# Attention of every tile in float32 quarters of the array, first mixture in blocks of 512 tokens, memory laid out anew

## The chip, the core and the metric

The kernel runs on one core of a Trainium2 chip. The metric is the device time of one execution in microseconds (us); smaller is better. The engines are named as in the profile: PE (TensorE, matmuls; PEld is its weight load), DVE (VectorE), ACT (ScalarE), POOL (GpSimd) and SP (SyncE, which here issues DMAs). Each has its own queue, worked off in order, and they meet at semaphores.

## The reference

Inputs and outputs are float32 in the reference. Three stages follow each other, for 8 x 576 = 4608 tokens of 512 features:

```python
# attention inside chunks of 64 tokens, 8 heads of 64
scores = scale * np.matmul(q_c, k_c.transpose(0, 1, 2, 4, 3))
scores = scores - np.max(scores, axis=-1, keepdims=True)
attn = np.exp(scores)
attn = attn / (np.sum(attn, axis=-1, keepdims=True) + 1e-09)
out = np.matmul(attn, v_c)
# first mixture: 512 -> 768 three times, the maximum of them, 768 -> 512
h = np.maximum(np.maximum(x @ w1, x @ w2), x @ w3)
x = h @ w_out
# second mixture: each token goes to one of 8 experts, 512 -> 1024 -> 512
e_idx = np.argmax(x @ w_gate, axis=1)
out[mask] = gate_w[mask, None] * eom[mask, e, None] * (np.maximum(x[mask] @ w1[e], 0.0) @ w2[e])
```

The gate's weight is the softmax's value at the chosen expert, `eom` a sigmoid of a second set of logits. The first mixture's four weight matrices reach the chip as float64 words.

## The kernel before, in words

**Tiles and blocks.** A tile is 128 tokens (two chunks of 64, all eight heads); there are 36. The first mixture takes three tiles together, as a block of 384 tokens; there are 12 blocks (`blocks`, line 62). The second mixture takes blocks of 256 tokens of one expert, gathered from a table in memory.

**Hi and lo.** A float32 matmul is made of three float32r ones: each operand is split in a hi part (an ACT copy that rounds) and a lo part (a subtraction on DVE or POOL), and `mm3` (lines 99 to 102) adds hi x hi, hi x lo and lo x hi. All matmuls of both mixtures are of this kind.

**Attention** has five steps per tile. `att_Q` loads q and k (SP) and, from tile 5 on, splits them: q into `qs`, k into `kb`, in which k stands as blocks so that one matmul does two heads and two chunks. `att_S` makes the scores. From tile 5 on these are four `mm3` of 128x256 columns, twelve matmuls, into the PSUM banks `a2` (line 427). Tiles 0 to 4 (`a < NF`) take plain float32 instead, in quarters of the array: 16 matmuls of 64x64, one per head and chunk (line 417), which need no parts. ACT then copies the scores to `e`, DVE and POOL take off the maximum, ACT takes the exponential, DVE sums, POOL multiplies by the inverse. `att_P` loads v (and splits it, from tile 5 on), transposes the probabilities on PE (four matmuls, line 465) and copies them to SBUF: to `pTF` in the first tiles, and to `pT` in hi and lo parts from tile 5 on (four ACT copies, four DVE subtractions). `att_V` makes the values in the same two ways (line 495 for quarters, line 508 for `mm3`), again in `a2`, and splits the result into `xt`, the first mixture's input (two `xt`, used by blocks in turn).

**First mixture.** `convert` (lines 529 to 548) turns one 512x128 part of a weight matrix from float64 words into hi and lo: an ACT operation, four DVE operations (lines 537, 539, 542, 544), an ACT copy and a POOL subtraction. There are 18 such parts (`conv_w`) and six of `moe_w_out` (`conv_o`, which also works out the gates' weights on PE). Three buffers `cy` are used in turn by all 24. The float64 words of the 18 parts are staged in `wst`, six at a time, which lies in the memory of `wo`, the converted `moe_w_out`. `moe_f` makes one of 18 groups of a block: 12 matmuls of 128x384 into one of three PSUM banks in turn; ACT and DVE form the maximum over three groups in `hs0`, and ACT and POOL split it into `ht[g]`. `moe_y` makes the outputs of a tile, in two halves of 18 matmuls (256 and 272 columns; the second with the gate's logits). `gate` works out the routing of a block, and `rows_out` writes the rows to the scratch tensor.

**Order.** All this is listed as operations with an engine, an estimated duration, a priority and the keys of the memory that they read and write. `order` (line 282) then runs a list schedule: each engine takes the most urgent operation that can start by the estimates, and that is the fixed order of its queue. So attention of block j + 1, the mixture of block j and the conversions are interleaved by priorities (`v0(j)` plus constants), and the dependencies follow the order of the list. Operations on a made-up engine `HOST` hand memory over: they come when all its old users are done.

**Second mixture.** Its first block is planned with the rest (`early_half`, `late_half`), the others follow in a written-out order (`step`). Buffers for the experts' weights (`raw`) take over the memory of attention, regions R0 to R3.

The lines that say it best are these two groups of the scores:

```python
for hp in range(HP):                       # tiles 0 to 4: 16 float32 matmuls
    add("PE", 0.44, pr + 1, [...], [...], lambda hp=hp: mm(hp))
...
for hp in range(HP):                       # tiles 5 to 35: 12 float32r matmuls
    add("PE", t_mm(256), pr + 1, ["qsh", "qsl"] + kbk, pk, lambda hp=hp: mm3(...))
```

## Time and profile before

| | us |
|---|---|
| median of 3 runs | 1287.7 |
| lowest and highest of them | 1287.33, 1288.24 |
| span of the profiled execution, first to last instruction | 1284.5 |
| busy: PE, DVE, ACT, POOL | 1236.8, 642.9, 523.2, 351.3 |
| first mixture with attention and conversion, by PE's timeline | 0 to 799.8 |
| second mixture | 799.8 to 1284.5 |

The profiled execution's own device time is not given apart; its span stands for it, 3.2 us under the median of the runs. A matmul's duration in the profile runs to its modelled end and overlaps the next one's; what one costs is the distance from its start to the next start. The busy time of PE therefore says only that it had something under way. Waits are told from the view that lists who waited for whom. A line number such as L97 or L100 is often that of a helper (97 is every subtraction, 100 to 102 the three matmuls of `mm3`); the tiles beside it tell which one is meant. Buffer numbers are left out: `a` is `a2`, `mm` any of three banks, `U` a region that several buffers share.

### The profile page before, as it was taken

To read this page: it belongs to the slowest core of one execution; us is meant where nothing else is said; L and a number is where in the kernel's file an instruction comes from. 1 tells how busy PE (TensorE), PEld (TensorE's weight loads), DVE (VectorE), ACT (ScalarE), POOL (GpSimd) and SP (SyncE) were. 2 spreads that over 40 slices of the span, in tenths; PEclk is the share of its full clock that TensorE was granted. 3 is DMA by queue.
4 is the path that set the end of the run, shared out by engine and by line. 5 is a ranking of instruction groups with operands and counts; after the bars stand their busy time and mean duration, and the time that the engine had idled before them with its cause. 6 is when DMAs were issued, how large, how long until landed. Compare 5 with 4: busy or idle time off the path is not lost. (4 is left out here: it accounts for less than half of the span.)

```text
span 1284.5 us, 22188 instructions
## 1 busy us (share of the span) xinstructions
PE 1236.8 (96%) x8450; PEld 1188.8 (93%) x8450; DVE 642.9 (50%) x1397; ACT 523.2 (41%) x1055; POOL 351.3 (27%) x376
## 2 busy tenths in 40 slices
...
PEclk7888999999999999999999999999999999999998
...
GB/s 284 194 97 84 65 27 75 33 68 50 50 59 42 66 34 75 25 75 26 75 9 35 131 25 41 199 34 54 47 107 200 216 59 34 115 108 42 59 162 29
DMA packets 54107, 102.98 MB, mean 80 GB/s; under 512 B 5983, under 2 KB 15199, under 8 KB 53984
## 3 DMA queue, kind: packets, MB, share of 16 engines
...
q14 instruction: 54, 0.44, 0.1%
...
## 5 line engine op out<-in xcount | busy, mean ns | idle before, releaser
L100 PE MATMUL mm<-xt,wpc 128*128 128x384 f32 x768 | 264.0, 344 | 2.1 <-DVE hs L616 1.9
L101 PE MATMUL mm<-xt,wpc 128*128 128x384 f32 x768 | 261.3, 340 | 3.2 <-DVE xt L97 3.2
L102 PE MATMUL mm<-xt,wpc 128*128 128x384 f32 x768 | 261.1, 340 | 0.0
L873 DVE SCALAR_TENSOR_TENSOR wo<-mm,wo 128x512 fp32r<-128x512 f32 x64 | 43.6, 689 | 238.6 <-ACT wo L869 191.9
L100 PEld LDWEIGHTS mm<-xt,wpc 128*128 128x128 f32 x768 | 145.8, 190 | 3.6 <-DVE hs L616 2.1
L101 PEld LDWEIGHTS mm<-xt,wpc 128*128 128x128 f32 x768 | 145.7, 190 | 3.6 <-DVE xt L97 3.6
L102 PEld LDWEIGHTS mm<-xt,wpc 128*128 128x128 f32 x768 | 145.5, 189 | 0.0
L97 POOL TENSOR_TENSOR ht<-hs,ht 128x384 fp32r<-128x384 f32 x72 | 74.4, 1033 | 255.5 <-ACT ht L618 254.6
L889 POOL DMA_INDIRECT out_dram<-yo,S x42 | 44.1, 1051 | 354.9 <-ACT yo L886 271.4
L616 DVE TENSOR_TENSOR hs<-mm,hs 128x384 f32<-128x384 f32 x144 | 80.1, 556 | 121.7 <-PE mm L102 117.2
L100 PE MATMUL mm<-wo,ht 128*128 128x256 f32 (+1 forms) x432 | 125.4, 290 | 0.0
L102 PE MATMUL mm<-wo,ht 128*128 128x256 f32 (+1 forms) x432 | 123.0, 285 | 0.0
L101 PE MATMUL mm<-wo,ht 128*128 128x256 f32 (+1 forms) x432 | 123.0, 285 | 0.0
L618 ACT CAST ht<-hs 128x384 fp32r<-128x384 f32 x72 | 36.9, 513 | 204.7 <-DVE hs L616 203.9
L100 PE MATMUL tr<-wpc,wo 128*128 128x512 f32 x304 | 120.3, 396 | 0.0
L102 PE MATMUL tr<-wpc,wo 128*128 128x512 f32 x304 | 118.6, 390 | 0.0
L101 PE MATMUL tr<-wpc,wo 128*128 128x512 f32 x304 | 118.5, 390 | 0.0
L97 DVE TENSOR_TENSOR pT<-tr,pT 64x256 fp32r<-64x256 f32 x124 | 52.3, 422 | 72.8 <-ACT pT L478 71.5
L869 ACT ACTIVATE wo<-mm 128x512 fp32r<-128x512 f32 x64 | 38.2, 597 | 122.5 <-PE mm L102 120.0
L886 ACT ACTIVATE yo<-tr,xg 128x512 f32<-128x512 f32 x42 | 28.5, 687 | 143.0 <-PE tr L102 143.0
L97 DVE TENSOR_TENSOR wpc<-raw,wpc 128x512 fp32r<-128x512 f32 x112 | 70.3, 685 | 30.7 <-ACT wpc L827 30.7
L101 PEld LDWEIGHTS mm<-wo,ht 128*128 128x128 f32 x432 | 81.8, 189 | 0.0
...
## 6 DMA issues: line engine op xcount, KB each, us to landing
...
```

Of the source, the lines that this page charges most:

```text
L97: eng.tensor_tensor(out=o, in0=a, in1=b, op=ALU.subtract)
L100: PE.matmul(o, ah, bh, start=first, stop=False)
L101: PE.matmul(o, ah, bl, start=False, stop=False)
L102: PE.matmul(o, al, bh, start=False, stop=last)
L616: add("DVE", t_dve(N), up, [pk, hk], [hk], lambda: DVE.tensor_tensor(out=h, in0=ps, in1=h, op=ALU.max))
L618: add("ACT", t_act(N), up, [hk], [("ht", g, 0)], lambda: ACT.copy(ht[g][:, 0, :N], h))
L869: ACT.activation(out=hT()[:, 0, 2 * c:2 * c + 2], in_=l1_ps(c), func=ACTF.Relu)
L873: DVE.scalar_tensor_tensor(out=hT()[:, 1, fs], in0=l1_ps(c), scalar=0.0, in1=f(hT()[:, 0, fs]), op0=ALU.max, op1=ALU.subtract)
L886: ACT.activation(out=yo(b, t), in_=ps_y[t], func=ACTF.Copy, scale=xg(b)[:, t, DM:DM + 1])
L889: POOL.indirect_dma_start(out=out, out_offset=bass.IndirectOffsetOnAxis(ap=ic[b % 4]()[:, t, 1:2].bitcast(U32), axis=0), in_=yo(b, t), in_ ...
```

## The change

All 36 tiles take attention in float32 quarters; the hi and lo parts of q, k, v and the probabilities, their buffers (`kb`, `pT`, `qs`, `vs`) and their clearing go, and PE's operation for a tile's scores or values is planned as one of 0.7 us. Blocks have four tiles, so that `moe_f` has 512 columns; there are nine. Memory is laid out anew: R0 to R3 hold q, k, v (three v buffers), three score buffers, two probability buffers and two of the three `cy`; `xt` is split into hi and lo tiles; the float64 words are staged, four parts at a time, in the place of the second `xt`, which is handed over (`HOST`) when all 18 parts are read; `wo` has its own memory from the start. The second mixture's `xs[0]` and other late buffers get new places of the same use. Priorities are set for the longer blocks (`VB`, `FD`, `YD`), and tiles 3 and 4 lose their own (`AF`). The rest of the diff removes comments.

```diff
-    blocks = [3] * 12
+    blocks = [4] * 9
...
     LP, LQ = -158, 8
-    AO, AS = -15, 14
+    AO, AS = -15, 16
-    AF, PS, VS, GP, YB = -40, 19, 0, 54, 1
+    AF, PS = -40, 19
+    VB, FD, YD = 76, 3.0, 56
...
-    NF, NE2, NW = 5, 3, 3
-    S0, S1, Q0, Q1, K0, K1, MULD = 2, 36, 0, 9, 3, 9, 2
+    NE2, NW = 3, 3
+    S0, S1, MULD = 2, 36, 2
...
-    kb = ar.tile([P, 2, 4, 2, P], F32R, tag="R0", name="kb")
-    pT = ar.tile([P, 2, 2, 4, P], F32R, tag="R1", name="pT")
-    qk_a = ar.tile([P, 2, 2, HP, P], F32, tag="R2", name="qk_a")
-    qkv_b = ar.tile([P, 4, HP, P], F32, tag="R3", name="qkv_b")
-    qk_buf = [qk_a[:, 0], qk_a[:, 1], qkv_b[:, 0:2]]
-    v_buf = [qkv_b[:, 2], qkv_b[:, 3]]
-    qvs = buf([P, 2, 2, 4, P], F32R, "qvs")
-    qs, vs = qvs[:, 0], qvs[:, 1]
-    e = buf([P, H, 64], F32, "e")
-    mxs, sms = ([buf([P, H], F32, f"{n}{i}") for i in range(4)] for n in ("mx", "sm"))
-    xt = [buf([P, 2, KD, TB * P], F32R, f"xt{i}") for i in range(2)]
+    rg = [ar.tile([P, 2048], F32, tag=f"R{n}", name=f"rg{n}") for n in range(4)]
+    part = lambda n, i, m: rg[n][:, i * 512:(i + m) * 512]
+    qk_buf = [part(n, i, 2).rearrange("p (w h t) -> p w h t", w=2, h=HP) for n, i in ((0, 0), (0, 2), (1, 0))]
+    v_buf = [part(n, i, 1).rearrange("p (h t) -> p h t", h=HP) for n, i in ((1, 2), (1, 3), (2, 3))]
+    es = [part(2, i, 1).rearrange("p (h j) -> p h j", h=H) for i in range(3)]
+    pTF = [part(3, i, 1).rearrange("p (a b c) -> p a b c", a=HP, b=2) for i in range(2)]
+    NV = len(v_buf)
+    xtn = lambda hl, i: f"xt{'hl'[hl]}{i}"
+    xtile = lambda hl, i: p1.tile([P, KD, TB * P], F32R, name=xtn(hl, i), tag=xtn(hl, i))
+    xt = [[xtile(hl, 0) for hl in range(2)], None]
+    wst = [p1.tile([P, 2, KD, P, 2], I32, name=f"wst{hl}", tag=xtn(hl, 1)) for hl in range(2)]
...
-    wst = wp.tile([P, 6, KD, P, 2], I32, tag="wo", name="wst")
-    wo_t = []
-    US = 4096
+    wo_t = [wp.tile([P, 2, NG, DM + 2 * E], F32R, tag="wo", name="wo")]
...
     so = [View(i * 1024, 1024, I32, "p (k f w) -> p k f w", k=KD, w=2) for i in range(2)]
-    cy = [View(2048 + i * 512, 512, I32, "p (k f) -> p k f", k=KD) for i in range(3)]
-    wT = [View(3584, 512, F32, "p (k f) -> p k f", k=KD)]
-    es = [e] + [View(o, 512, F32, "p (h j) -> p h j", h=H) for o in (3584, 1024, 1536)]
-    pTF = [View(i * 512, 512, F32, "p (a b c) -> p a b c", a=HP, b=2) for i in range(2)]
+    wT = [View(2048, 512, F32, "p (k f) -> p k f", k=KD)]
+    cyv = View(2560, 512, I32, "p (k f) -> p k f", k=KD)
+    cy = [(cyv.ap, cyv)] + [
+        (part(3, 2 + i, 1).bitcast(I32).rearrange("p (k f) -> p k f", k=KD), ("cy", i)) for i in range(2)
+    ]
...
     def e_of(a):
-        i = a % NE2 if a < NF else 0
-        return (es[i].ap if i else e), [es[i] if i else ("e", 0), ("mx", i), ("sm", i)], mxs[i], sms[i]
+        i = a % NE2
+        return es[i], [("e", i), ("mx", i), ("sm", i)], mxs[i], sms[i]
...
+    T_Q = 0.7
     def att_Q(a, pr):
-        t = qk_buf[a % 3]
         for w in range(2):
             load(a, w, pr - LA)
-        if a < NF:
-            return
-        add("ACT", t_act(512), pr, [("qk", a % 3, 0)], ["qsh"], lambda: ACT.copy(qs[:, 0], t[:, 0]))
-        add_sub(lo((Q0, Q1), a), 512, pr, [("qk", a % 3, 0), "qsh"], ["qsl"], qs[:, 1], t[:, 0], f(qs[:, 0]))
-        for h2 in range(2):
-            sl = h64(h2)
-            add("ACT", t_act(512), pr, [("qk", a % 3, 1)], [("kbh", h2)],
-                lambda sl=sl, h2=h2: ACT.copy(kb[sl, 0, :, h2], t[sl, 1]))
-        for h2 in range(2):
-            sl = h64(h2)
-            add_sub(lo((K0, K1), a), 512, pr, [("qk", a % 3, 1), ("kbh", h2)], [("kbl", h2)],
-                    kb[sl, 1, :, h2], t[sl, 1], f(kb[sl, 0, :, h2]))
...
     def att_S(a, pr):
         e, (ek, mk, sk), mx, sm = e_of(a)
-        if a < NF:
...
+        t = qk_buf[a % 3]
+        bank = [ps[:, i] for ps, _, hs in quarters(a) for i in range(hs.stop - hs.start)]
+        def mm():
+            for hp in range(HP):
                 for h2 in range(2):
                     for c in range(2):
                         x = t[h64(h2), :, hp, h64(c)]
                         PE.matmul(bank[h2][h64(c), hp], x[:, 0], x[:, 1], start=True, stop=True)
...
-        else:
-            kbk = [("kbh", 0), ("kbh", 1), ("kbl", 0), ("kbl", 1)]
-            pk = ["a2"]
-            sc = ps_a2.rearrange("p (a h c j) -> p a h c j", a=HP, h=2, c=2)
-            for hp in range(HP):
...
-            for c in range(2):
-                sl = h64(c)
-                add("ACT", t_act(512), pr + 1, pk + ([ek] if c else []), [ek] if c == 0 else [("e", 1)],
-                    lambda sl=sl, c=c: ACT.copy(e[sl], sc[sl, :, :, c, :].rearrange("p a h j -> p (a h) j")))
-        add("DVE", t_dve(512), pr + 1, [ek, ("e", 1)], [mk], lambda: DVE.tensor_reduce(out=mx, in_=e, axis=AX.X, op=ALU.max))
+        add("PE", T_Q, pr + 1, [("qk", a % 3, 0), ("qk", a % 3, 1)], [x for _, kk, _ in quarters(a) for x in kk], mm)
+        for ps, pk, hs in quarters(a):
+            add("ACT", t_act(256 * (hs.stop - hs.start)), pr + 1, pk + ([ek] if hs.start else []), [(ek, 1)] if hs.start else [ek],
+                lambda ps=ps, hs=hs: ACT.copy(e.rearrange("p (a b) j -> p b a j", b=2)[:, hs], ps))
+        ek2 = [ek, (ek, 1)]
+        add("DVE", t_dve(512), pr + 1, ek2, [mk], lambda: DVE.tensor_reduce(out=mx, in_=e, axis=AX.X, op=ALU.max))
...
     def att_P(a, pr):
         e, (ek, _, _), _, _ = e_of(a)
         load(a, 2, pr - LV)
-        vv = v_buf[a % 2]
-        if a >= NF:
-            add("ACT", t_act(512), pr + 6, [("v", a % 2)], ["vsh"], lambda: ACT.copy(vs[:, 0], vv))
-            add("POOL", t_pool(512), pr + 6, [("v", a % 2), "vsh"], ["vsl"], lambda: sub(POOL, vs[:, 1], vv, f(vs[:, 0])))
         pp = ps_tr[a % 2].rearrange("p (a c i) -> p a c i", a=HP, c=2)
 
...
-        add("PE", 0.43, pr + 2, [ek], [("tr", a % 2)], fn)
+        add("PE", 0.45, pr + 2, [ek], [("tr", a % 2)], fn)
         x = pTF[a % 2]
-        d = lambda hl, c, h2: x.ap[h64(c), :, h2] if a < NF else pT[h64(c), hl, h2, :, 64 * c:64 * c + 64]
         for i, (c, h2) in enumerate((c, h2) for c in range(2) for h2 in range(2)):
-            kf = [x, ("pTF", a % 2, 0)] if i == 0 else [("pTF", a % 2, i)]
-            add("ACT", t_act(256), pr + 2, [("tr", a % 2)] + ([("pTF", a % 2, 0)] if a < NF and i else []),
-                kf if a < NF else [("pth", c, h2)],
-                lambda c=c, h2=h2: ACT.copy(d(0, c, h2), pp[h64(h2), :, c]))
-        for c in range(2) if a >= NF else ():
-            for h2 in range(2):
-                add_sub("DVE", 256, pr + 2, [("tr", a % 2), ("pth", c, h2)], [("ptl", c, h2)],
-                        d(1, c, h2), pp[h64(h2), :, c], f(d(0, c, h2)))
+            add("ACT", t_act(256), pr + 2, [("tr", a % 2)], [("pTF", a % 2, i)],
+                lambda c=c, h2=h2: ACT.copy(x[h64(c), :, h2], pp[h64(h2), :, c]))
...
     def att_V(a, pr):
         j, t_ = tile_block[a]
-        dst = xt[j % 2][:, :, :, t_ * P:(t_ + 1) * P]
+        dst = lambda hl: xt[j % 2][hl][:, :, t_ * P:(t_ + 1) * P]
         xk = lambda hl: [("xt", j % 2, t_, hl, h2) for h2 in range(2)]
...
+        vv, x = v_buf[a % NV], pTF[a % 2]
+        bank = [ps[:, i] for ps, _, cs in quarters(a) for i in range(cs.stop - cs.start)]
+        def mm():
+            for hp in range(HP):
                 for c in range(2):
                     for h2 in range(2):
-                        PE.matmul(bank[c][h64(h2), hp], vv[h64(c), hp, h64(h2)], x.ap[h64(c), hp, h2], start=True, stop=True)
...
-            return
-        ptk = [(x, c, h2) for x in ("pth", "ptl") for c in range(2) for h2 in range(2)]
-        pk = ["a2"]
-        pv = ps_a2.rearrange("p (a h c) -> p a h c", a=HP, h=2)
-        for hp in range(HP):
-            add("PE", t_mm(256), pr + 3, ["vsh", "vsl"] + ptk, pk, lambda hp=hp: mm3(
-                pv[:, hp], vs[:, 0, hp], vs[:, 1, hp], pT[:, 0, :, hp], pT[:, 1, :, hp], True, True,
-            ))
-        for h2 in range(2):
-            sl = h64(h2)
-            add("ACT", t_act(512), pr + 3, pk, [xk(0)[h2]], lambda sl=sl, h2=h2: ACT.copy(dst[sl, 0], pv[sl, :, h2]))
-        for h2 in range(2):
-            sl = h64(h2)
-            add_sub("DVE", 512, pr + 3, pk + [xk(0)[h2]], [xk(1)[h2]], dst[sl, 1], pv[sl, :, h2], f(dst[sl, 0]))
+                        PE.matmul(bank[c][h64(h2), hp], vv[h64(c), hp, h64(h2)], x[h64(c), hp, h2], start=True, stop=True)
+        add("PE", T_Q, pr + 3, [("v", a % NV)] + [("pTF", a % 2, i) for i in range(4)], [x for _, kk, _ in quarters(a) for x in kk], mm)
+        o = lambda hl: dst(hl).rearrange("p a (b i) -> p b a i", b=2)
+        for ps, pk, cs in quarters(a):
+            n = 256 * (cs.stop - cs.start)
+            kx = lambda hl: [("xt", j % 2, t_, hl, i) for i in range(cs.start, 2)] if n == 256 else xk(hl)
+            add("ACT", t_act(n), pr + 3, pk, kx(0), lambda ps=ps, cs=cs: ACT.copy(o(0)[:, cs], ps))
+            add("DVE", t_dve(n), pr + 3, pk + kx(0), kx(1), lambda ps=ps, cs=cs: sub(DVE, o(1)[:, cs], ps, f(o(0)[:, cs])))
...
     def conv_w(n, pr):
         g, w = divmod(n, 3)
-        t = wst[:, n % 6]
-        tk = [("wo", 2 * (n % 6)), ("wo", 2 * (n % 6) + 1)]
+        t = wst[n % 4 // 2][:, n % 2]
+        tk = [("ws", n % 4)]
         add("SP", 1.46, min(pr - 25, LP + LQ * n), [], tk, lambda: SP.dma_start(
...
-        pc, x = wpc[n // 4], xt[j % 2]
+        pc, x = wpc[n // 4], lambda: xt[j % 2]
         for kk in range(KD):
             add("PE", t_mm(N), pr, [("w", n, 0), ("w", n, 1)] + xt_keys(j), [pk], lambda kk=kk: mm3(
                 ps, pc[:, 0, n % 4, kk], pc[:, 1, n % 4, kk],
-                x[:, 0, kk, :N], x[:, 1, kk, :N], kk == 0, kk == KD - 1), lead=0.1)
+                x()[0][:, kk, :N], x()[1][:, kk, :N], kk == 0, kk == KD - 1), lead=0.1)
...
     def v0(j):
-        return 25 + 64 * j
+        return 25 + VB * j
...
     akeys = [
-        [(x, h2) for x in ("kbh", "kbl") for h2 in range(2)],
-        [(x, c, h2) for x in ("pth", "ptl") for c in range(2) for h2 in range(2)],
         [("qk", i, w) for i in range(2) for w in range(2)],
         [("qk", 2, 0), ("qk", 2, 1), ("v", 0), ("v", 1)],
+        [x for i in range(3) for x in (("e", i), (("e", i), 1))] + [("v", 2)],
+        [("pTF", i, x) for i in range(2) for x in range(4)] + [("cy", i) for i in range(2)],
     ]
...
     def attention(a, n):
         def prio(i):
             j, t = tile_block[i]
-            return -100 + PS * i if j == 0 else AF + AO + AS * i if i < NF else v0(j - 1) + AO + AS * t
+            return -100 + PS * i if j == 0 else v0(j - 1) + AO + AS * t
...
-            if i == NA - 1 and VS:
-                att_V(i, pr[i])
             if i + 1 < NTILE:
                 att_S(i + 1, pr[i + 1])
-            if i != NA - 1 or not VS:
-                att_V(i, pr[i])
-    add("POOL", 1.7, -60, [], [(x, h2) for x in ("kbh", "kbl") for h2 in range(2)], lambda: zero(POOL, kb))
-    add("POOL", 1.7, -55, [], [(x, c, h2) for x in ("pth", "ptl") for c in range(2) for h2 in range(2)], lambda: zero(POOL, pT))
-    NA = max(NF, blocks[0])
+            att_V(i, pr[i])
+    NA = blocks[0]
     attention(0, NA)
     for n in range(NFT):
         conv_w(n, v0(0) + CW * n - CO)
     add("SP", 0.5, 0, [], ["gwr"], gw_load, lat=LD)
-    add("HOST", 0.0, 0, [], [("wo", i) for i in range(2 * NG)],
-        lambda: wo_t.append(wp.tile([P, 2, NG, DM + 2 * E], F32R, tag="wo", name="wo")))
+    add("HOST", 0.0, 0, [], [("ws", i) for i in range(4)] + xkeys(1, 0, 1),
+        lambda: xt.__setitem__(1, [xtile(hl, 1) for hl in range(2)]))
     for i in range(NG):
         conv_o(i, v0(0) + CP + i)
...
         for n in range(NFT):
-            moe_f(j, n, base + 2.75 * n)
+            moe_f(j, n, base + FD * n)
         if j == NB - 1:
-            early_half(base + 44)
-        for i, half in enumerate((0, 1) if j < YB else (1, 0)):
+            early_half(base + YD - 6)
+        for i, half in enumerate((0, 1) if j == 0 else (1, 0)):
             for t in range(blocks[j]):
-                moe_y(j, t, half, base + 50 + 2.2 * t + 6.6 * i)
+                moe_y(j, t, half, base + YD + 2.2 * t + 8.8 * i)
             if half:
-                gate(j, base + GP + 6.6 * i)
-        rows_out(j, base + 60)
-    late_half(pe_ + 62)
+                gate(j, base + YD + 4 + 8.8 * i)
+        rows_out(j, base + YD + 12)
+    late_half(pe_ + YD + 12)
     for o in order():
         o.fn()
```

## Rows read from the trace of the kernel before

**Rows 1.** Page, part 2, PEclk: granted TensorE clock in tenths, 40 equal slices of the span.
```profile
PEclk7888999999999999999999999999999999999998
```
**Rows 2.** Busy time by stretch: PE, PEld, DVE, ACT, POOL (records), granted clock, DMA share, GB/s.
```profile
30.00:122.00 92.00, 69.90 (x452) 65.70 (x450) 88.58 (x128) 49.95 (x95) 59.40 (x46) 0.87 0.41 135
...
136.00:800.00 664.00, 663.60 (x4431) 661.07 (x4431) 377.53 (x961) 294.78 (x641) 173.05 (x185) 1.00 0.16 51
```
**Rows 3.** PE's waits, 130 to 860 us, all of them: total us, times, longest.
```profile
PE a L845 <- DMA xg<-x_scratch,S: 0.4, 1, 0.4
```
**Rows 4.** Timeline of PE: start, us, instruction; block 0, block 1, second mixture.
```profile
35.52 0.69 PE L101 MATMUL mm<-xt,wpc 128*128 128x384 f32 x1 [3.17 <-DVE xt L97]
...
135.46 0.34 PE L100 MATMUL mm<-xt,wpc 128*128 128x384 f32 x1
...
799.76 0.28 PE L100 MATMUL mm<-qvs,wpc 128*128 128x256 f32 x1
```
**Rows 5.** Timeline of PE, first and last of 118 such starts in block 11.
```profile
760.05 0.34 PE L100 MATMUL mm<-xt,wpc 128*128 128x384 f32 x1
...
780.64 0.34 PE L100 MATMUL mm<-xt,wpcr 128*128 128x384 f32 x1
```
**Rows 6.** Timeline of PE, second mixture: first of 23 512-column matmuls, next start behind them.
```profile
818.66 0.40 PE L101 MATMUL tr<-wpc,wo 128*128 128x512 f32 x1
...
823.91 0.28 PE L100 MATMUL mm<-wo,wpc 128*128 128x256 f32 x1
```
**Rows 7.** Timeline of PE: first of twelve matmuls of a tile's scores, next start.
```profile
300.91 0.28 PE L100 MATMUL a<-kb,qvs 128*128 128x256 f32 x1
...
302.34 0.29 PE L100 MATMUL mm<-wo,ht 128*128 128x272 f32 x1
```
**Rows 8.** Timeline of PE around tile 3's values, in quarters.
```profile
43.76 0.34 PE L102 MATMUL mm<-xt,wpc 128*128 128x384 f32 x1
44.03 0.69 PE L495 MATMUL a<-U,qkv_b 64*64 64x64 f32 x32
44.65 0.66 PE L465 MATMUL tr<-ident,U 128*128 128x128 f32 x4
45.06 0.42 PE L100 MATMUL mm<-xt,wpc 128*128 128x384 f32 x1
```
**Rows 9.** Timeline of PE: tile 4's values, with the wait before them.
```profile
64.06 1.14 PE L495 MATMUL a<-U,qkv_b 64*64 64x64 f32 x32 [4.95 <-ACT e L439]
```
**Rows 10.** Timeline of DVE: last step of weight 17, and of the last part of moe_w_out.
```profile
92.51 0.68 DVE L544 SCALAR_TENSOR_TENSOR U<-wst,U 128x512 int32<-128x512 int32 x1
...
120.87 0.69 DVE L544 SCALAR_TENSOR_TENSOR U<-U 128x512 int32<-128x512 int32 x1
```
**Rows 11.** Instructions of line 539: ns at the shortest, in the median, at the longest.
```profile
L539 DVE TENSOR_SCALAR U<-U x24: 409/1138/1510, 12.2 to 117.9; 128x512 int32<-128x512 int32 x24
```
**Rows 12.** Groups of DVE, 0 to 122 us: busy us, mean ns, idle before.
```profile
L539 DVE TENSOR_SCALAR U<-U 128x512 int32<-128x512 int32 x24 | 23.2, 974 | 0.1
L537 DVE TENSOR_SCALAR U<-U 128x512 f32<-128x512 f32 x24 | 17.2, 728 | 3.0 <-ACT U L536 3.0
L544 DVE SCALAR_TENSOR_TENSOR U<-wst,U 128x512 int32<-128x512 int32 x18 | 16.3, 905 | 0.0
L542 DVE SCALAR_TENSOR_TENSOR U<-wst,U 128x512 int32<-128x512 int32 x18 | 15.7, 877 | 0.1
```
**Rows 13.** Groups of POOL, 0 to 122 us.
```profile
L97 POOL TENSOR_TENSOR kb<-qk_a,kb 64x512 fp32r<-64x512 f32 x4 | 5.6, 1406 | 0.2
L97 POOL TENSOR_TENSOR qvs<-qkv_b,qvs 128x512 fp32r<-128x512 f32 x3 | 4.4, 1470 | 0.4 <-ACT qvs L459 0.3
```
**Rows 14.** Busy time of PE alone, in block 11's outputs: length, busy (records), clock, DMA, GB/s.
```profile
785.20:792.80 7.60, 7.60 (x63) 1.00 0.24 65
```
**Rows 15.** Timeline of PE: the gate's two small matmuls in block 11.
```profile
794.54 0.18 PE L671 MATMUL psg<-ohz,tri 128*128 128x32 bf16 x1
794.57 0.18 PE L672 MATMUL psg<-ohc,ones_b 128*128 128x32 bf16 x1
```

58 lines of the change are left out of this document (17 added, 41 removed).

## The prediction

> **What bounds the kernel now.** I read the page's slices first, then the busy time by stretch, then the tensor engine's waits, and last its timeline, where costs are taken from start to start, because the durations of pipelined matmuls overlap. The granted clock is below full only in the first slices and the last [rows 1]. By stretch there are two regimes. From 136 to 800 us PE is busy 663.6 of 664.0 us at clock 1.00 while DVE works 377.5, ACT 294.8 and POOL 173.1 us [rows 2], and the list of PE's waits from 130 to 860 us holds one entry, 0.4 us [rows 3]: there only PE's own work counts. From 30 to 122 us it is the other way round: DVE is busy 88.6 of 92 us, PE 69.9 at a granted clock of 0.87 [rows 2] (a mixture of the 1.2 and the 2.4 GHz level). That is the conversion of the float64 weights, which feeds block 0. Block 0's matmuls run from 35.5 us, block 1 begins at 135.46 and the second mixture at 799.76 us [rows 4]. What follows 799.76 (484.7 us) does the same instructions after the change and I leave it as it is.
>
> So there are two accounts: PE's work from block 1 to the second mixture, and the time at which block 1 can begin.
>
> **First mixture in blocks of 512.** The columns stay the same, the number of matmuls falls from 12 x 216 = 2592 to 9 x 216 = 1944. A 384-column matmul starts every 20.59 us / 117 = 0.176 us [rows 5]. The change's 512-column one has its price in the second mixture, which does the same kind of float32r matmul: (823.91 - 818.66) / 23 = 0.2283 us [rows 6]. Per tile of 128 tokens: 72 x 0.176 = 12.67 us before, 54 x 0.2283 = 12.33 after, so 0.34 us less, 12 us over all 36 tiles. The output matmuls (moe_y) keep their shapes. The gate loses one small pair per merged block, under 0.3 us in all. PSUM: 512 float32 columns fill a bank, and three banks still rotate. The chain that frees hs0 for the next group (DVE maximum, ACT copy, POOL subtraction) was never waited for at 384 columns [rows 3], and it grows by a third as the matmuls do that hide it, so I put no wait there.
>
> **Attention in quarters.** Today 31 of 36 tiles (a >= 5) take twelve 128x256 matmuls for the scores and as many for the values: 302.34 - 300.91 = 1.43 us for one dozen [rows 7], 2.86 per tile. The quarter form is in the trace already, for the first five tiles. Amid full-width matmuls at full clock one group of 16 (32 records) runs from 44.03 to the next transposes at 44.65, 0.62 us, and its entry costs 0.09 (44.03 - 43.76 = 0.27 instead of 0.176) [rows 8]: 0.71 with both edges, 1.42 for scores and values, 1.44 less per tile, 45 us over 31 tiles. Bounds: 0.62 per group if the entry is hidden; 1.14 for the group at 64.06 [rows 9], which ran behind a stall at a lower granted clock. I take 0.71, because its neighbours are those of the steady stretch.
>
> What goes from the other engines in the steady stretch (hi and lo copies and subtractions of q, k, v and the probabilities) is covered by PE throughout and costs or gains nothing there. If this cover were thin, DVE with its 378 of 664 us would be next; its load falls too.
>
> A rule that speaks against this: the Trainium skill, "TensorE: Matmul & The Clock Gate", section "Wait — 56ns, not 53.3ns?", says that from start to start a matmul never takes under some 25 ns however short it is. By that figure a group would be an estimate of 32 x 0.025 + 0.09 = 0.89 us and the gain 11 us smaller; the row of 32 records in 0.62 us goes below it, 0.0194 each [rows 8], and I keep the row.
>
> **The start.** What is removed from DVE before the conversions end (the last one starts its last operation at 120.87 us [rows 10]): four pT subtractions and, as the values of tiles 4 to 6 now wait, two or three xt subtractions, at an estimate of 0.4 and 0.7 us each from the unstretched operations of 512 elements [rows 10, 11]; against them block 0's 12 maxima grow by a third. Net some 2 us. More is in DVE's stretched operations: L539 takes 0.409 us at its shortest and 1.138 in the median [rows 11], and L537, L539, L542 and L544 together hold 17.2 + 23.2 + 15.7 + 16.3 = 72.4 us [rows 12] where 84 instructions at 0.41 to 0.69 us would take 45: some 28 us are stretch, at times when POOL works. POOL, busy 59.4 us from 30 to 122 [rows 2], loses six kb and five qvs subtractions of 1.4 to 1.5 us there (four and three of them in [rows 13]), some 16 us, a quarter. A quarter of 28 is 7 us. So the conversions end 9 us earlier, at an estimate of 112 us. Bounds: 0 (other POOL work takes the slots) and 20 us.
>
> The order of the conversions stays: the three cy buffers go round in the order of the list, so wo's six parts still come behind weight 15. What the new layout does change is xt[1], which is staging memory until weight 17 is read; the values of tiles 4 to 7 wait for that. Today weight 17 gives its memory back at 93.2 us, 28 before the last conversion [rows 10], so four groups of 0.71 us and their evictions have room, beside the conversion of wo. Block 0 itself needs four tiles instead of three and should start near 39 us; its 18 groups of 12 x 0.2283 = 2.74 us are 49.3 us of PE, done by 90 to 95, in time for wo. Behind the last conversion stand today 135.46 - 120.87 = 14.6 us until block 1: the gate products and the rest of block 0's outputs. The fourth tile adds 36 output matmuls at 7.6 / 63 = 0.1206 us [rows 14], 4.3 us. So block 1 begins at 112 + 14.6 + 4.3 = 131 us, 4.5 earlier than today although with four tiles behind it instead of three. Bounds: 140 (conversions no earlier) and 120 (20 earlier, which is also about what PE's own work needs: 39 + 49.3 + 17.4 of outputs + some 13 of attention and gate products). The weights' loads run 4 ahead instead of 6; at 4 us per weight that is still 16 us, the DMA share from 30 to 122 us is 0.41 [rows 2], and SP's queue keeps its order, so nothing for that.
>
> **The sum.** Before: 664.3 us from 135.46 to 799.76 are 33 tiles of the mixture and 30 of attention at 2.86 + 0.41 (transposes, 45.06 - 44.65 [rows 8]) = 3.27, so 17.16 us per tile of the mixture. After: 32 tiles at 17.16 - 0.34 = 16.82 and 28 of attention at 1.42 + 0.41 = 1.83: 538.2 + 51.2 = 589.5 us. The second mixture begins at 131 + 589.5 = 720.5 instead of 799.76, 79 us earlier: 12 from the blocks, 45 from attention, the rest, 22, from the start, where a tile more is done by an earlier time. The page gives the profiled execution by its span, 1284.5 us; the median of the three runs, 1287.7, lies 3.2 above it, which I carry over: 1287.7 - 79.2, about 1209 us. Its own range: start 120 to 140 (-11, +9), groups 0.62 to 1.14 over 56 groups (-5, +24); not all together, so 1196 to 1234.
>
> **Rivals.**
> Late values. For it: the values, evictions and probabilities of tiles 6 and 7 form a chain with two pTF buffers behind xt[1], and block 1 needs the last of it. Against: 28 us of wo's conversion and 17 of outputs lie beside it. If the chain (an estimate of 4 us per tile, from copies and subtractions of 0.4 to 0.7 us) came behind the outputs, block 1 would start 16 us later: 1225 us. Chance 0.12.
> A floor on starts. If a quarter matmul started no faster than the shortest full-width matmul in the steady stretch, 0.03 us (794.57 - 794.54 [rows 15]), a group would take 32 x 0.03 + 0.09 = 1.05 us and the time would be 1209 + 62 x 0.34 = 1230. The Trainium skill's floor, told above, is of this kind. Against: row 8's 0.62. Chance 0.05.
> Cover gone. Another engine, or the in-order queues, take over as PE gets faster, so that the 45 us of attention don't come out: 1254. Against: every other engine is at 57% or less in the steady stretch [rows 2] and loses work. Chance 0.05.
> The other side: the shared bank a2. Scores of one tile and values of another use it in turn, and at 64.06 the values waited 4.95 us for ACT to clear the scores [rows 9]. If the planner, which now takes 0.7 us for a whole group, puts the two so close that each of the 28 tiles pays this, that is 140 us: 1349. It decides from 79 / 28 = 2.8 us per tile on. Against: the same bank served both in the steady stretch, with no wait [rows 3]. Chance 0.03.
> That the change doesn't do what it says (block 0 or some tiles keep the old form) I can exclude from the code.
>
> **How the numbers follow.** Forecast 0.72, late values 0.12, floor 0.05, cover 0.05, bank 0.03, others 0.03. The likeliest is 1209 us. The range takes in its own bounds, the late values and the floor: 1196 to 1234. A measurement of this kernel tells 0.2% (2.6 us) from no change; only the bank and part of the rest miss that: faster 0.95, same 0.01, slower 0.04.
>
> **What would show it.** Right: quarter groups 0.6 to 0.75 us from start to start in the steady stretch; 512-column matmuls every 0.228 us; block starts about 74 us apart; POOL free of kb and qvs; DVE's L539 shorter in the mean; the conversions over near 112 us, block 1 at about 131, the second mixture at about 720, and 485 us behind it. Wrong: PE waits in the steady stretch on ACT for a2 or on xt; a start of block 1 after 140; groups above 1.1 us; a second mixture that takes longer than 485.

## The result: 1229.86 us, 0.956 of the time before

| | before | after |
|---|---|---|
| median, us (lowest and highest) | 1287.51 (1286.47 to 1288.24) | 1229.86 (1228.77 to 1230.34) |
| ratio, 95% interval | 1 | 0.9557, 0.9543 to 0.9570 |
| span of the profiled execution | 1284.5 | 1227.0 |

The kernel is faster, as forecast, and the time lies in the range (1196 to 1234), but 21 us above the forecast of 1209. Where the profile after differs from the plan is found by the same views in the same order.

The page of the changed kernel, parts 1 and 2: busy times, and the granted clock in 40 slices. The clock is below full in the first slices and the last, as in [rows 1], and DVE, ACT and POOL have lost 180, 117 and 70 us.

```profile
PE 1189.1 (97%) x9127; PEld 1039.6 (85%) x9127; DVE 462.9 (38%) x1056; ACT 406.3 (33%) x827; POOL 281.7 (23%) x313
...
PEclk8889999999999999999999999999999999999998
```

Busy time by stretch (PE, PEld, DVE, ACT, POOL with records; clock, DMA share, GB/s), which answers to [rows 2]: the start, and the steady stretch, in which PE is now busy every microsecond. PE's waits from 122 to 860 us are an empty list, so none of the rivals that put a wait there came true.

```profile
30.00:122.00 92.00, 76.34 (x565) 60.53 (x566) 81.58 (x128) 47.44 (x89) 49.95 (x40) 0.91 0.43 140
142.00:740.00 598.00, 598.00 (x4783) 505.77 (x4782) 204.92 (x604) 181.16 (x415) 123.26 (x136) 1.00 0.17 56
```

The timeline of PE (start, us, instruction) gives the same marks as [rows 4], and one more: the last matmul of block 0's groups, behind which its outputs begin.

```profile
40.91 0.50 PE L101 MATMUL mm<-xth,wpc 128*128 128x512 f32 x1 [1.66 <-ACT xth L466]
...
120.66 0.40 PE L103 MATMUL mm<-xth,wpcr 128*128 128x512 f32 x1
120.89 0.28 PE L101 MATMUL mm<-wo,ht 128*128 128x256 f32 x1
...
140.47 0.39 PE L101 MATMUL mm<-xth,wpc 128*128 128x512 f32 x1
...
740.15 0.28 PE L101 MATMUL mm<-xs,wpc 128*128 128x256 f32 x1
```

Block 1 begins at 140.47 us (131 forecast, 135.46 before) and the second mixture at 740.15. Behind that mark 18 output matmuls of the last block still run, 2.2 us, so 742.4 is the mark to set beside the 799.76 of before. The steady stretch takes 742.4 - 140.47 = 601.9 us (589.5 forecast, 664.3 before), and what follows it 484.6 us (484.7 before). The miss is thus +9.5 us at the start and +12.4 in the steady stretch, and nothing in the second mixture.

**The steady stretch.** Timeline of PE after, a scores group between two matmuls of 512 columns, and 27 starts of such matmuls in a row (305.96 to 312.21):

```profile
305.96 0.39 PE L103 MATMUL mm<-xth,wpc 128*128 128x512 f32 x1
...
312.21 0.40 PE L103 MATMUL mm<-xth,wpc 128*128 128x512 f32 x1
312.54 0.69 PE L409 MATMUL a<-rg 64*64 64x64 f32 x32
313.16 0.50 PE L101 MATMUL mm<-xth,wpc 128*128 128x512 f32 x1
313.50 0.39 PE L102 MATMUL mm<-xtl,wpc 128*128 128x512 f32 x1
```

Inside, the group takes 313.16 - 312.54 = 0.62 us, as in [rows 8]. In front of it the last full-width matmul holds PE for 0.33 instead of 0.23, the 0.09 that I had counted. Behind it, the first full-width matmul holds PE for 313.50 - 313.16 = 0.34: a second edge of 0.11 that [rows 8] could not show, because there transposes follow the group. Over all 56 groups the means are 0.094 + 0.625 + 0.109 = 0.83 us where I had 0.71. A 512-column matmul starts every 6.25 / 27 = 0.231 us here, 0.2304 in the mean over the stretch, where [rows 6] gave 0.2283.

The Trainium skill, TensorEngine Tiling (Array Packing), section Key Properties, says that a change of the tiling mode (not of the tile alone) drains TensorE; it gives no price. The rows agree in that a change costs time, 0.09 us on the way in and 0.11 on the way out; that a drain is what costs it, no run here shows.

**The start.** Timeline of DVE after: the last operation of the last conversion, which answers to [rows 10]. It ends at 112.3 us; 112 was forecast.

```profile
111.65 0.68 DVE L493 SCALAR_TENSOR_TENSOR rg<-U,rg 128x512 int32<-128x512 int32 x1
```

The four largest waits of PE after, 35 to 145 us (us in total, times, longest):

```profile
PE psg L523 <- DVE U L493: 5.7, 1, 5.7
PE mm L101 <- ACT xth L466: 1.7, 1, 1.7
PE mm L101 <- ACT hs L563: 1.5, 1, 1.5
PE tr L437 <- POOL rg L427: 1.4, 1, 1.4
```

The longest has this place in PE's timeline: the transposes of the first gate product stand in the queue ahead of groups 12 to 17.

```profile
80.94 0.39 PE L103 MATMUL mm<-xth,wpc 128*128 128x512 f32 x1
87.06 1.12 PE L523 MATMUL psg<-ident,U 128*128 128x128 f32 x4 [5.73 <-DVE U L493]
```

The conversions end as forecast, but behind them 28.1 us pass until block 1, not 18.9: 8.6 until the last group of block 0 is done (120.9), and 19.6 for its 144 outputs, none of which ran earlier. Before the change the groups were over 20 us ahead of the last conversion, as PE's timeline of before shows, and 37 of the 108 outputs too:

```profile
101.27 0.33 PE L102 MATMUL mm<-xt,wpcr 128*128 128x384 f32 x1
...
103.76 0.28 PE L100 MATMUL mm<-wo,ht 128*128 128x256 f32 x1
```

### The profile page after: what moved, and what is told of

Read it like the earlier page. It is cut to its first block, busy times and chain, and to the rows that moved or that the text cites. A ratio compares the mean times of both kernels' runs of the same rounds, so it can differ in the third digit from the quotient of the medians.

```text
span 1227.0 us, 22763 instructions
## 1 busy us (share of the span) xinstructions
PE 1189.1 (97%) x9127; PEld 1039.6 (85%) x9127; DVE 462.9 (38%) x1056; ACT 406.3 (33%) x827; POOL 281.7 (23%) x313
## 5 line engine op out<-in xcount | busy, mean ns | idle before, releaser
L101 PE MATMUL mm<-xth,wpc 128*128 128x512 f32 x576 | 236.2, 410 | 3.7 <-ACT xth L466 1.7
L103 PE MATMUL mm<-xth,wpc 128*128 128x512 f32 x576 | 227.1, 394 | 0.0
L102 PE MATMUL mm<-xtl,wpc 128*128 128x512 f32 x576 | 226.5, 393 | 0.2 <-DVE xtl L98 0.2
L565 DVE TENSOR_TENSOR hs<-mm,hs 128x512 f32<-128x512 f32 x108 | 74.5, 690 | 214.2 <-PE mm L103 214.2
L101 PEld LDWEIGHTS mm<-xth,wpc 128*128 128x128 f32 x576 | 108.6, 189 | 28.1 <-ACT hs L563 1.9
L98 POOL TENSOR_TENSOR ht<-hs,ht 128x512 fp32r<-128x512 f32 x54 | 70.0, 1296 | 269.1 <-ACT ht L567 269.1
L103 PEld LDWEIGHTS mm<-xth,wpc 128*128 128x128 f32 x576 | 108.9, 189 | 25.3
L102 PEld LDWEIGHTS mm<-xtl,wpc 128*128 128x128 f32 x576 | 108.9, 189 | 20.5 <-DVE xtl L98 0.5
L103 PE MATMUL tr<-wpc,wo 128*128 128x512 f32 x304 | 118.5, 390 | 0.0
L101 PEld LDWEIGHTS mm<-wo,ht 128*128 128x128 f32 x432 | 81.2, 188 | 1.3
L102 PEld LDWEIGHTS mm<-wo,ht 128*128 128x128 f32 x432 | 81.4, 189 | 0.4
L103 PEld LDWEIGHTS mm<-wo,ht 128*128 128x128 f32 x432 | 81.3, 188 | 0.0
L101 PE MATMUL mm<-xs,wpc 128*128 128x256 f32 x272 | 76.7, 282 | 0.5 <-PEq L1106 0.3
```

Source lines behind the costliest of these rows:

```text
L98: eng.tensor_tensor(out=o, in0=a, in1=b, op=ALU.subtract)
L101: PE.matmul(o, ah, bh, start=first, stop=False)
L102: PE.matmul(o, ah, bl, start=False, stop=False)
L103: PE.matmul(o, al, bh, start=False, stop=last)
L565: add("DVE", t_dve(N), up, [pk, hk], [hk], lambda: DVE.tensor_tensor(out=h, in0=ps, in1=h, op=ALU.max))
```

## The experiments

All are timed against the kernel before, and told by ratio. 0.0020 of a ratio is 2.6 us. The changed kernel stands at 0.9557.

**Blocks of 384 with all else kept** (e1).

```diff
-    blocks = [4] * 9
+    blocks = [3] * 12
-    VB, FD, YD = 76, 3.0, 56
+    VB, FD, YD = 58, 2.5, 45
```

Buffers stay as large as for four tiles, and the other priorities are scaled alike.

> The changed kernel with blocks of three tiles again (moe_f of 384 columns, 12 blocks, priorities scaled to them), everything else of the change kept. Theory (the matmuls' start distances): 72 x 0.176 - 54 x 0.2304 = 0.23 us per tile, 8 us over 36 tiles, so about 1238 us; block starts in the steady stretch 57 us apart. Rival 1 (longer blocks also pay at the start, because each converted weight feeds more columns): 8 + some 10 us, about 1248. Rival 2 (512 columns gain nothing, since they start every 0.2304 us and not 0.2283): 1230 to 1232.

Measured: 1237.5 us, ratio 0.9633 (0.9617 to 0.9649). That is the theory's 1238 us. The larger blocks bring 0.0076, 9.8 us (12 forecast); attention, memory and start together 3.7%, 47 us. The 9.8 is not all the matmuls': in e1 a 384-column start takes 0.1748 us in the mean, so they give 72 x 0.1748 - 54 x 0.2304 = 0.14 us per tile, 5 us over 36 tiles, and the blocks agree with that (57.65 us apart, 19.22 per tile, against 76.3 and 19.08). The ratios leave some 2.7 us either way, and the profiled executions lie only 7.2 us apart; where the rest comes from isn't shown. Block 1 begins at 122.72 us, with three tiles behind it; the last conversion ends at 108.3, 14.4 earlier. The fourth tile thus costs the start 140.47 - 122.72 = 17.8 us, while a tile of the steady stretch takes 601.9 / 32 = 18.8. That is one point at which the forecast went wrong: I had let the fourth tile into the start for nearly nothing.

**Every quarter group twice** from tile 8 on (e2).

```diff
-            for hp in range(HP):
+            for hp in [*range(HP)] * (2 if a >= 8 else 1):
```

> The changed kernel, with the 16 quarter matmuls of the scores and of the values issued twice in a row from tile 8 on (the same result twice). 56 groups. Theory (PE is the bound, a group costs 0.5 us for its 32 records and 0.3 for its edges): 56 x 0.5 = 28 us more, 1258. Rival 1 (other engines or waits hide the groups): no change, 1230. Rival 2 (the edges are small and the whole 0.83 us lies in the records): 56 x 0.8 = 45 us more, 1275.

Measured: 1257.39 us, 0.9783 (0.9767 to 0.9799), 29 us more than the changed kernel, as the theory had it. Timeline of PE in this kernel, a doubled group of 64 records:

```profile
306.53 0.40 PE L103 MATMUL mm<-xth,wpc 128*128 128x512 f32 x1
306.86 1.16 PE L409 MATMUL a<-rg 64*64 64x64 f32 x64
307.95 0.50 PE L101 MATMUL mm<-xth,wpc 128*128 128x512 f32 x1
308.29 0.39 PE L102 MATMUL mm<-xtl,wpc 128*128 128x512 f32 x1
```

The second sixteen add 0.47 us and the edges stay 0.33 and 0.34. So a group has a price of its own and a price for its two borders with full-width matmuls, and both are PE's alone: 56 groups cost all that they last, and nothing hides them.

**Values of a tile and scores of the next as one group** from tile 8 on, the values in the other halves of the banks of `a2` (e4).

```diff
-        add("PE", T_Q, pr + 3, [("v", a % NV)] + [...], [...], mm)
+        if pre:
+            add("PE", 1.3, pr + 3, rd + pre[0], wr + pre[1], lambda: (pre[2](), mm()))
+            att_S(a + 1, pre[3], True)
+        else:
+            add("PE", T_Q, pr + 3, rd, wr, mm)
```

> The changed kernel with the values of tile i and the scores of tile i + 1 as one operation of PE from tile 8 on, the values in the other halves of a2's two banks. Theory (each entry into and exit from a quarter group costs 0.10 and 0.11 us besides the records): 27 pairs of edges fall away, 27 x 0.21 = 6 us less, up to 10 if the drain between the two goes too: 1220 to 1224. Rival 1 (the edges are not on the path): 1230. Rival 2 (the scores now wait for the probabilities of the tile before, and PE waits in the steady stretch): above 1232.

Measured: 1220.46 us, 0.9503 (0.9487 to 0.9519): **faster than both kernels**, and than the changed one by 0.0054, 7 us. Timeline of PE in it:

```profile
316.12 0.40 PE L103 MATMUL mm<-xth,wpc 128*128 128x512 f32 x1
316.45 0.69 PE L410 MATMUL a<-rg 64*64 64x64 f32 x32
316.96 0.65 PE L464 MATMUL a<-rg,rg 64*64 64x64 f32 x32
317.54 0.50 PE L101 MATMUL mm<-xth,wpc 128*128 128x512 f32 x1
317.88 0.39 PE L102 MATMUL mm<-xtl,wpc 128*128 128x512 f32 x1
```

One way in (0.33) and one way out (0.34) for 64 records in 1.09 us. Against two groups of 0.83 this saves 2 x 0.83 - (0.094 + 1.092 + 0.109) = 0.36 us, 27 times: 9.9 us; the second mixture begins 8.25 us earlier (731.90), and the rest of the 9.9 isn't accounted for. Of the 0.36, 0.20 is the pair of borders. The other 0.16 lies inside the group, which pays it once: as in e2, the first sixteen matmuls take 0.625 us and the second sixteen 0.47.

**The planner's durations as measured** (e3): 0.0155 us beside the columns for a matmul, 0.83 for a group, 0.72 to 0.95 for DVE's conversion steps.

```diff
-        return k * (0.0025 + n / 2400)
+        return k * (0.0155 + n / 2400)
-    T_Q = 0.7
+    T_Q = 0.83
```

> The changed kernel with the planner's durations set to what the trace shows (matmul 0.0155 us + columns / 2400, a group 0.83, the four DVE steps of a conversion 0.72, 0.95, 0.88 and 0.88 us); no work changes, only the order of the queues. Theory (block 0 is late because PE's fixed order puts transposes of moe_w_out ahead of groups that are ready, 6.1 us at 81): block 1 starts up to 6 us earlier, 1224 us. Rival 1 (the conversions set block 1's start whatever the order): 1230. Rival 2 (the order gets worse elsewhere): above 1232.

Measured: 1229.65 us, 0.9564 (0.9547 to 0.9580), no change, and the theory falls. Block 0's groups are done by 111.7 instead of 120.89, but the last conversion ends at 125.2, and block 1 begins at 140.77. What PE's order gained, DVE's order gave back.

**PE's queue re-ordered** (e9, e5, e8). Seven operations of three matmuls, of groups 11 to 13, go ahead of the transposes at which PE stood from 81 to 87 us (`first`); `fs` are block 0's matmul operations, `isf` tells them.

```diff
+    for o in plan:
+        due += 7 * (o is first) + isf(o)
+        while due and fs and fs[0].need <= done:
+            due -= 1
+            done.add(fs[0])
+            seq.append(fs.pop(0))
+        if not isf(o):
+            seq.append(o)
+            done.add(o)
```

In e5 `isf` took in the matmuls of every block, and what was still due behind block 0 pulled matmuls of each later block ahead of the outputs.

> The changed kernel with PE's queue alone re-ordered in block 0: seven operations (21 matmuls) of groups 11 to 13 come before the transposes of the first part of moe_w_out, for which PE stood idle 6.1 us at 81 us; the orders of DVE, ACT and POOL stay. Theory (PE's fixed order is what is wrong with the predicted start): the idle time falls from 6.1 to about 2 us, block 0's groups are done by about 116 instead of 120.9, block 1 starts near 136 instead of 140.5, and the time is 1225.5 us where the changed kernel has 1229.9. Rival (DVE's order holds the start: the maxima of the groups stand between the conversions, and three PSUM banks let PE run no further ahead): PE gets its idle time back a few groups later, waiting for DVE's maxima; block 1 at 139.5 to 141, time 1229 to 1230.

Measured: 1253.24 us, 0.9752 (0.9702 to 0.9801), 25 us slower than the changed kernel. The edit reached further than was meant, so the time says nothing of block 0 (its trace does, below); the blocks are 78.6 us apart instead of 76.3, and PE now waits for DVE's maxima between them (214 to 600 us: five waits, 1.7 us). The rest of the difference I haven't taken apart. e9 does it in block 0 alone:

> The changed kernel with PE's queue alone re-ordered, and this time in block 0 alone: seven operations (21 matmuls) of groups 11 to 13 come before the first gate product's transposes, at which PE stood idle 6.1 us; all other orders stay. Theory (PE's order costs part of block 0's idle time): PE's idle times over 0.6 us from 40.9 us to block 1, 12 us together in the changed kernel, fall to some 8; groups done by about 116 instead of 120.9, block 1 at 136 to 138 instead of 140.5, time 1225.5 to 1227.5 where the changed kernel has 1230. Rival (the rest of block 0 waits for DVE and ACT, whose order stays): block 1 at 139.5 to 141, time 1229 to 1230.5.

Measured: 1232.69 us, 0.9575 (0.9550 to 0.9599). By ratio that is not to be told from the changed kernel. The profiled execution is the slowest of four (1229.19 to 1234.31). In it, groups are done 2.4 us earlier (118.5), yet block 1 comes 3.7 us later (144.21). Busy time by stretch in e9 (columns as above):

```profile
78.00:90.00 12.00, 9.26 (x69) 6.51 (x68) 11.90 (x17) 5.01 (x9) 7.44 (x5) 1.00 0.15 46
110.00:120.00 10.00, 7.55 (x28) 5.91 (x28) 2.97 (x8) 2.74 (x6) 2.67 (x4) 0.70 0.01 2
120.00:130.00 10.00, 9.71 (x54) 9.71 (x55) 1.64 (x4) 2.07 (x5) 1.39 (x2) 0.61 0.00 0
```

The same stretches in the changed kernel:

```profile
78.00:90.00 12.00, 6.27 (x53) 4.65 (x52) 11.90 (x18) 6.24 (x12) 7.53 (x5) 0.73 0.13 44
110.00:120.00 10.00, 9.52 (x55) 8.15 (x55) 4.33 (x11) 3.77 (x8) 2.91 (x6) 1.00 0.01 2
120.00:130.00 10.00, 10.00 (x127) 9.50 (x129) 1.38 (x2) 2.31 (x5) 1.71 (x2) 1.00 0.07 24
```

The idle time at 81 us is smaller, and the granted clock stays at 1.00 there. But idle time comes back at 110 us, where PE has little left and waits for DVE's maxima and the last gate products (28 records in 10 us against 55), and there the clock falls: 0.70 and 0.61 in the two stretches, a mixture of its levels of 1.2 and 2.4 GHz, and the outputs run at it. The gap was moved, not filled.

The clock didn't have to fall, though. In block 0 e5 has the same order of PE, and the same gap at 110 us; its stretches from 110 to 130 us:

```profile
110.00:120.00 10.00, 7.49 (x49) 6.44 (x50) 3.96 (x10) 3.20 (x6) 2.77 (x5) 1.00 0.01 2
120.00:130.00 10.00, 9.99 (x134) 9.39 (x133) 2.19 (x4) 3.68 (x8) 2.33 (x2) 1.00 0.22 70
```

There the groups are done by 116.2, as the theory had it, and block 0's outputs at 144.47, with 21 matmuls of block 1 (4.8 us) pulled in among them: about 139.6 without these. That is the rival's number (139.5 to 141). So at full clock the new order brings block 1 forward by an estimated 1 us, and what lies above it in e9's trace came with the lower clock, which one execution had and the other had not.

e8 lets the planner do it, by a later priority of the gate products on PE:

```diff
-        add("PE", 0.43, pr, [yk], ["psg"], tr)
+        add("PE", 0.43, pr + 33 + 2 * i, [yk], ["psg"], tr)
-        add("PE", 0.5, pr, [w, "gwr"], ["psg"], mm)
+        add("PE", 0.5, pr + 33 + 2 * i, [w, "gwr"], ["psg"], mm)
```

> The changed kernel with the planner's priority of the gate products on PE set later (by 33 + 2 i for part i), so that the list schedule itself puts groups 11 to 13 first; here DVE's order changes with it: the maxima and two steps of attention move ahead of some conversions of moe_w_out. Theory (PE's order and DVE's order must both give way): idle time at 81 us mostly gone, groups done near 115, conversions 1 to 3 us later than 112.3, block 1 near 136, time 1225. Rival (the conversions' end alone sets the start): block 1 as much later as the conversions are, 141 to 143, time 1230 to 1232.

Measured: 1228.02 us, 0.9546 (0.9521 to 0.9571), not to be told from the changed kernel. Groups done at 117.4, conversions at 113.1, block 1 at 139.68; the 6 us at 81 are still idle, now for the scores, which wait for DVE's subtraction of the values before them. Neither theory's number came out; both orders hold PE at that place.

**Joined groups and the re-ordering together** (e6 with the edit that reached too far, e11 with the one in block 0).

> The kernel with joined groups (ratio 0.9503 to the kernel before) with the same re-ordering of PE's queue. If the two gains add and the theory of the re-ordering holds: 1219 us, ratio 0.947. If the re-ordering gives nothing: 1223.5, ratio 0.950.

> The kernel with joined groups with block 0's re-ordered PE queue. If the gains add and the theory of the re-ordering holds: ratio 0.947 to 0.949 to the kernel before (1219.5 to 1221.5 us where the kernel before has 1287). If the re-ordering gives nothing: 0.950 (1223).

Measured: 0.9666 (0.9646 to 0.9686) and 0.9535 (0.9517 to 0.9553): both worse than the joined groups alone, as the re-ordering alone gained nothing either. In e11 the clock is 0.66 from 120 to 130 us. With joined groups PE's long wait is another one, 6.7 us for DVE's subtraction of a tile's values, in e4 and e11 alike; the re-ordering doesn't reach it, so these two runs say little on its theory.

**POOL's share in the conversions** (e10, e7). POOL makes the lo part of weights 3 to 13 twice.

```diff
-        add("POOL", ..., lambda: sub(POOL, w(1), yf, f(w(0))))
+        add("POOL", ..., lambda: [sub(POOL, w(1), yf, f(w(0))) for _ in range(2 if 3 <= c < 14 else 1)])
```

In e7 the condition named another variable (`n` for `c`) and added nothing, so its instructions are those of the changed kernel:

> The changed kernel, in which POOL makes the lo part of weights 3 to 13 twice (11 subtractions of 128x512 more, about what the removed kb and qvs subtractions were, 16 us of POOL); the planned durations and all orders stay. Theory (POOL's work stretches DVE's conversion steps, and taking it away gave the predicted 7 us): the four conversion steps, which take 78.7 us together in the changed kernel and 84.8 in the one before, go back to about 85, and the last conversion ends 6 to 8 us later, near 118 to 120 instead of 112.3; block 1 starts 4 to 7 us later, time 1234 to 1237. Rival (the stretch does not come from POOL; the earlier end comes from the work that DVE lost): the steps stay within 1 us of 78.7, the end within 2 us of 112.3 and the time within 2 us of 1229.9.

It is therefore a second measurement of the changed kernel, 1230.16 us, 0.9554 (0.9528 to 0.9580). e10 is the experiment:

> The changed kernel, in which POOL makes the lo part of weights 3 to 13 twice: 11 subtractions of 128x512 more, 16 us of POOL, about what the removed kb and qvs subtractions were; all other orders stay. Theory (a conversion step on DVE lasts longer when POOL works beside it, and taking POOL work away gave the predicted 7 us): the four conversion steps, 78.7 us together in the changed kernel and 84.8 in the one before, go back to 84 to 87, the last conversion ends 6 to 9 us later than 112, block 1 3 to 7 us later than 140.5, time 1233 to 1237. Rival (POOL is not the cause): the steps stay within 1 us of 78.7, the end within 2 us of 112, time 1228 to 1232.

Measured: 1240.42 us, 0.9641 (0.9623 to 0.9659), 10.8 us more by ratio. Busy time by stretch in this kernel: POOL has 62 us where the changed kernel has 50.

```profile
30.00:122.00 92.00, 71.58 (x504) 55.69 (x505) 86.18 (x118) 44.19 (x84) 61.97 (x45) 0.83 0.43 138
```

The largest group of DVE's conversion steps in it, 0 to 125 us (busy us, mean ns, idle before):

```profile
L491 DVE SCALAR_TENSOR_TENSOR rg<-wst,rg 128x512 int32<-128x512 int32 x12 | 13.5, 1134 | 0.1
```

And its timelines of DVE and PE, the last step of the last conversion and block 1's first matmul:

```profile
122.27 0.68 DVE L493 SCALAR_TENSOR_TENSOR rg<-U,rg 128x512 int32<-128x512 int32 x1
...
151.09 0.39 PE L101 MATMUL mm<-xth,wpc 128*128 128x512 f32 x1
```

The same group takes 10.2 us, 853 ns each, in the changed kernel. All four steps together: 84.8 us before the change, 78.7 after, 87.4 here. 16 us of POOL stretch DVE's steps by 8.7 us, its idle time up to there grows by 1.4, and the last conversion comes 10.6 us later, and block 1 with it by 10.6. The distance from the one to the other stays 28.1.

How a single step shows it: line 488 in the changed kernel, 0 to 122 us, in ns at the shortest, in the median and at the longest.

```profile
L488 DVE TENSOR_SCALAR rg<-rg x16: 408/424/1540, 20.0 to 109.0; 128x512 int32<-128x512 int32 x16
```

The twelve of its 24 operations (both buffers) beside which POOL does nothing, or works for less than 60 ns, take 408 to 427 ns; the twelve beside POOL 505 to 1540, 1176 in the mean. The Trainium skill, SBUF — State Buffer, section Who interferes with whom, says that DVE (in its two-port modes, or with two inputs from SBUF) and GpSimd share a port pair as a lock, held for a whole instruction, while the other stands. The trace agrees: beside POOL the operation is longer by anything up to 1540 - 420 = 1120 ns, about the length of one of POOL's (1.0 to 1.75 us), as a wait for its end would be.

**Conversions without their first step on DVE** (e12): the limiting of the weights to float32's range is left out.

```diff
-        add("DVE", ..., lambda: DVE.tensor_scalar(
-            out=yf, in0=yf, scalar1=F64_MIN, scalar2=F64_MAX, op0=ALU.max, op1=ALU.min))
+        add("DVE", ..., lambda: None)
```

> The changed kernel without the first of the four conversion steps on DVE (the limiting of the weights to float32's range is left out; 24 operations, 19.5 us of DVE before block 1); the order of all that stays is kept. Together with the doubled POOL work (conversions 10.6 us later, block 1 10.6 later) it shows on both sides what sets the start of block 1. Theory (DVE's conversions pace block 0, its matmuls included, until PE's own work takes over: block 0's matmuls, attention, gate products and outputs are some 86 us of PE at full clock from 41 us on, so about 127 us): conversions over at 93 to 98 us, block 1 at 127 to 131 instead of 140.5, time 1217 to 1221. Rival 1 (block 1 stays the same distance behind the last conversion, without a floor): block 1 at 121 to 126, time 1211 to 1215. Rival 2 (PE's fixed order holds the start whatever DVE does): block 1 within 3 us of 140.5, time 1227 to 1231.

Measured: 1224.50 us, 0.9523 (0.9507 to 0.9539). Its timelines of DVE and PE, the last step of the last conversion and block 1's first matmul:

```profile
106.74 0.68 DVE L493 SCALAR_TENSOR_TENSOR rg<-U,rg 128x512 int32<-128x512 int32 x1
...
135.51 0.39 PE L101 MATMUL mm<-xth,wpc 128*128 128x512 f32 x1
```

Two of DVE's waits in it up to the last conversion, 0 to 107.4 us (us in total, times, longest):

```profile
DVE mx L416 <- ACT rg L414: 7.7, 4, 5.1
DVE wo L535 <- PE psg L531: 2.5, 3, 1.3
```

The same two in the changed kernel, 0 to 112.3 us:

```profile
DVE mx L416 <- ACT rg L414: 5.8, 3, 5.0
DVE wo L535 <- PE psg L531: 0.2, 1, 0.2
```

DVE's work shrank by 13.0 us (78.7 to 65.7; the steps that stay are stretched more), yet the conversions end only 4.9 us earlier. Up to the last one DVE is busy for 10.3 us less (90.2 instead of 100.5) and idle for 5.4 more (17.2 instead of 11.9): it waits longer for ACT's copies in attention, and 2.3 us longer for the gate products that PE has in its queue between groups. Block 1 follows at the same distance, 135.51 - 107.42 = 28.1. So the first rival's rule holds and its numbers don't, since the conversions weren't as free to move as all three theories took them to be.

## Why the prediction was right, and where it was off

**What bounds the kernel: right.** PE in the steady stretch, the conversions at the start; no wait of PE from 122 us on. The rival of the shared bank `a2`, which stood for the other side, is out with that (no wait at all), as are the late values and the lost cover. The floor on starts is out too: 32 records in 0.62 us are 0.0195 each in the steady stretch, so here the Trainium skill's floor of some 25 ns (TensorE: Matmul & The Clock Gate, section "Wait — 56ns, not 53.3ns?") does not hold for quarter matmuls. By it, the doubled group of e2 would have added 0.80 us instead of 0.47.

**First mixture in blocks of 512: right in kind, a little too large.** 12 us forecast; by the starts of before and after it is 72 x 0.176 - 54 x 0.2304 = 0.23 us per tile, 8 us over all (9.8 by e1, with all that differs there). The term that was mis-sized is the 512-column start: 0.2304 instead of 0.2283, 32 tiles x 54 x 0.0021 = 3.6 us. Why this matmul is slower by 2 ns here than the same one in the second mixture is open. It isn't slower at times when ACT or DVE read PSUM (0.2303 with, 0.2304 without), and with 384 columns and the new memory (e1) a start takes 0.1748, not more than the 0.176 of [rows 5].

**Attention in quarters: right in kind, 0.71 should have been 0.83.** The step that failed is "0.71 with both edges": [rows 8] shows one edge against a full-width matmul, the way in, and I took the way out into transposes for the general case. 56 x 0.109 = 6.1 us. The group's own mean adds 0.5. With the 3.6 above these are 10.2 of the 12.4 us; 2.2 I can't place. The transposes hold none of it: between full-width matmuls, with their own way out, they take 0.438 us now and 0.449 before, so the forecast's 0.41 was too low on both sides of its sum.

**The start: the forecast of the conversions held, that of block 1 did not.** Conversions over at 112 was forecast, 112.3 measured. The reason given for it holds as well: 2 us of work that DVE lost and 7 from POOL's lost work. Up to the last conversion DVE's other work shrank by 2.6 us and its idle time stayed (11.7 before, 11.9 after), the steps shrank by 6.1 and, the other way round, 11 more POOL operations stretched them by 8.7. What failed is the sentence that block 0's groups would be "done by 90 to 95, in time for wo". I had taken 18 x 2.74 = 49.3 us of PE as if nothing else ran. But block 0's groups stand in one queue with gate products, attention and waits. In the trace of before the same groups took from 35.52 (their second matmul; the first stood alone at 31.66) to 101.44, 66 us for 216 x 0.176 = 38 us of matmuls: 28 us in between. After the change it is 40.91 to 120.89, 80 us for 50: 30 in between. Had I read that row, 41 + 50 + 28 = 119 and my 17.4 for the outputs (19.6 as measured) would have given 136 to 139 for block 1. So "a tile more is done by an earlier time" was wrong: the fourth tile lies behind the last conversion in full, because the cover that I named, groups and outputs beside the conversion of wo, was already used up.

**That the time lies in the range is in part luck.** The start used up its whole allowance: it came at 140.47, beyond its bound of 140, and a start after 140 was one of the prediction's own signs of being wrong. The 12 us of the steady stretch fell into room that was made for something else, groups of 1.14 us at a lower granted clock, which never came (0.625 us each).

**What sets block 1 now.** With PE's order kept, the start follows the last conversion at 28.1 us, whether that is pushed back (e10) or drawn forward (e12). But it isn't the last conversion that releases PE. PE's longest wait behind 80 us is for DVE's conversion of the first part of `moe_w_out`, which the first gate product's transposes need. They start at 87.06 in the changed kernel; in e10 and in e12:

```profile
96.07 1.11 PE L523 MATMUL psg<-ident,U 128*128 128x128 f32 x4 [5.74 <-DVE U L493]
81.79 1.12 PE L523 MATMUL psg<-ident,U 128*128 128x128 f32 x4 [5.25 <-DVE U L493]
```

From there to block 1 PE works off its queue in 53.4, 55.0 and 53.7 us, with 0.8, 0.5 and 0 us of waits. So what moves this one conversion moved block 1, and the last conversion came along with it. That is also why e12 gained so little: this release came only 5.3 us earlier. With another order the distance is another (14.4 in e1, 15.6 in e3, 32.2 in e9), but new waits, the conversions or the clock took back what it gained, and block 1 stayed between 139.7 and 144.2 in e3, e8 and e9. DVE waits for PE's gate products, and PE for DVE's conversions and maxima. An order that fills PE's 6 us at 81 without opening a gap later was not found.
